# Full-width summary scores and another order of the first batch in a sparse-attention and mixture-of-experts kernel

## The chip, the core and the metric

The kernel runs on one core of a Trainium2 chip. The metric is device time in microseconds of one execution. Of several executions the median is taken.

## The reference

Two layers follow each other. The first is sparse attention with 4 batches, 8 heads, 768 positions and a head dimension of 64. Each query sees the keys that are less than 16 positions away, and in addition one summary of each block of 32 positions: the summary key is the maximum over the block, the summary value is the mean, and log 32 is added to its score.

```python
k_sum = k.reshape(B, H, nb, 32, D).max(axis=3)      # 24 summaries per head
v_sum = v.reshape(B, H, nb, 32, D).mean(axis=3)
scores_l = scale * q @ k.T                           # kept where |i - j| < 16
scores_s = scale * einsum('bhsd,bhnd->bhsn', q, k_sum) + log(32)
a = softmax(concat([scores_l_masked, scores_s]))
x = a @ concat([v, v_sum])                           # then (3072, 512)
```

The second is a mixture of 8 experts, each of them applied to all 3072 tokens and weighted by a routing matrix P that eight Sinkhorn steps make out of `exp(x @ w_gate)`.

```python
for e in range(8):
    out += P[:, e:e+1] * (relu(x @ w1[e]) @ w2[e])   # 512 -> 1024 -> 512
```

## The kernel before

Attention goes by pairs of heads: 16 pairs, four to a batch. A pair is one group of 128 partitions (two heads of 64). The first batch is cut into halves of 384 positions: four pairs, first halves, then the same four pairs, second halves (`pair_half`). The twelve pairs of the other batches are done whole (`pair_whole`). Between the attention work the kernel puts the products of expert 0 (`hidden0`, L211, and `project0`, L216), which need only the positions that are done. After the last attention come the Sinkhorn steps and experts 1 to 7, whose products follow Strassen's scheme (L764 and L815) with sums of weights, of tokens and of hidden values made on VectorE.

The steps of a pair, with the letter that the orders below use for its first half and the line of the profile:

- T, Q: keys and queries are transposed on TensorE (L300, L303, L312). k, q: the copies out of PSUM (L207), on ScalarE or VectorE.
- m: the key maxima over blocks of 32 on VectorE (L335, 128x24).
- v, V: block sums of the values on TensorE (L357) and their copy on VectorE (L363).
- S, X, b: scores of the near keys on TensorE (L347, in 64-row tiles), their exponentials on ScalarE (L490 for halves, L408 for whole pairs) and the band mask on VectorE (L495 and L500, or L412).
- s, e: summary scores on TensorE and their exponentials on ScalarE (L472).
- A, n: the products with the values on TensorE (L512 for halves, L435 and L441 for whole pairs) and the normalisation on VectorE (L542, L543).
- t, x: the transposition of the result (L550) and its copy to `xT` (L207).

Digits are the pair's number in its batch. F is a filler of zeros on TensorE; further fillers (`FILL`) are written into the first steps of v, S and s.

Summary scores have three forms. `summaries` for first halves uses 64x32 tiles (L452). For second halves it uses one matmul with all 128 columns of `ksT` (L455), where VectorE's `key_max_split` (L341) has put the maxima of the two heads into columns 0 to 63, each head's at its own 64 rows and zeros elsewhere, and columns 64 to 127 are zero. `summaries_2`, for the twelve whole pairs, runs two matmuls of 64 columns and 384 queries each, one for each half of the queries, into partitions 0 to 63 and 64 to 127 of one bank (L461). `summary_exp` then reads each half into rows 0 to 63 of `E_e`.

PSUM has three banks under tag "m" (products of expert 0, and the first halves' transpositions and summaries), three under "a" (the other attention steps) and one pair of banks under "s" (scores).

What sets the order: each step is added to a planner (`Plan`) with an engine or a choice of engines, a cost in microseconds, its dependencies, its buffers and a priority. `order` places the steps one after another where they can start first, and the program is written in that order, so that every engine's queue is fixed. Where a step may run on ScalarE or VectorE, the planner chooses. For the first halves of the first batch the order on TensorE, VectorE and ScalarE is written out by hand and made binding with `follow`:

```python
for u, d in zip(units, [None] + units):
    u.eng = {eng: u.eng[eng]}
    if d is not None:
        u.deps.append(d)
```

Of the kernel before, what the change touches and what calls it, by code (L numbers as in the profile page):

```python
# [10 lines left out]
BF16 = mybir.dt.bfloat16  # L11
# [117 lines left out]
def kernel(  # L129
# [10 lines left out]
    nc = tc.nc  # L140
# [12 lines left out]
    W = 16  # L153
    LIVE = 128 + 2 * W
    PADL = LIVE + 2 * W
    HS = S // 2
# [64 lines left out]
    NB = PB  # L221
# [4 lines left out]
    with tc.manual_schedule():  # L226
        attn = stage.enter_context(tc.tile_pool(name="attn", bufs=1))
# [10 lines left out]
        qT = [attn.tile([128, W + S + W], BF16, name=f"qT{i}") for i in range(NB)]  # L238
        kT = [attn.tile([128, S], BF16, name=f"kT{i}") for i in range(NB)]

        ks = [attn.tile([128, 1, 32], BF16, name=f"ks{i}") for i in range(NB)]
        ksT = [attn.tile([128, 128], BF16, name=f"ksT{i}") for i in range(NB)]
        v_x = [attn.tile([128, 2, G, VD], BF16, name=f"vx{i}") for i in range(NQ)]

        E_h = [attn.tile([128, 2, HG + 1, PADL], BF16, name=f"Eh{i}") for i in range(NEH)]
# [16 lines left out]
        def bank(tag, name, dtype=FP32):  # L262
            pool, n = (mps, 3) if tag == "m" else (aps, NA)
            return pool.tile([128, 2048 // mybir.dt.size(dtype)], dtype, tag=tag, name=name, bufs=n)
# [73 lines left out]

        def key_max_split(i):
            r = i % NB  # L340
            nc.vector.tensor_tensor(out=ksT[r][:, 0:64].rearrange("p (j n) -> p j n", j=2),  # L341
                                    in0=ks[r][:].to_broadcast([128, 2, 32]),
                                    in1=own[:].to_broadcast([128, 2, 32]), op=ALU.mult)

# [99 lines left out]
        def summaries(i, h, tag):  # L444
            r = i % NB
            ss, rhs = bank(tag, "ss"), qT[r][:, W + h * HS:W + (h + 1) * HS]
            wait_busy("s", i, h, ss)
            at["ss", i, h] = ss
            if i < PB and not h:
                for j in range(2):  # L450
                    p = slice(64 * j, 64 * j + 64)
                    nc.tensor.matmul(ss[32 * j:32 * j + 32, 0:HS], lhsT=ks[r][p, 0, :], rhs=rhs[p],  # L452
                                     start=True, stop=True)
                return
            nc.tensor.matmul(ss[:, 0:HS], lhsT=ksT[r][:], rhs=rhs, start=True, stop=True)  # L455

        def summaries_2(i):
            r, ss = i % NB, bank("a", "ss")
            for h in range(2):
                at["ss", i, h] = ss[64 * h:64 * h + 64]  # L460
                nc.tensor.matmul(ss[64 * h:64 * h + 64, 0:HS], lhsT=ksT[r][:, 0:64],  # L461
                                 rhs=qT[r][:, W + h * HS:W + (h + 1) * HS], start=True, stop=True)

        def summary_exp(i, h):
            if i < PB:
# [155 lines left out]
        def wait_busy(what, i, h, t):  # L621
            for _ in range(FILL.get(what + str(i), 0) if i < PB and not h else 0):
                stream(t, 512)
# [29 lines left out]
        def constants():  # L653
            nc.vector.memset(warm, 0.0)
            nc.scalar.dma_start(out=wg_f32[:], in_=moe_w_gate.rearrange("(dk p) e -> p dk e", p=128))
            nc.scalar.activation(out=warm[:], in_=warm[:], func=AF.Exp, bias=0.0, scale=1.0)
            for t in qT:
                nc.vector.memset(t[:, 0:W], 0.0)
                nc.vector.memset(t[:, W + S:], 0.0)
            for t in qT:  # L660
                nc.vector.memset(t[:, W + HS:W + HS + W], 0.0)
            for t in ks:
                nc.vector.memset(t[:, 0, 24:32], 0.0)
            for t in ksT:
                nc.vector.memset(t[:, 64:128], 0.0)
            for t, n in ((own, 64), (own_n, 32)):
                nc.vector.memset(t, 0.0)
                for j in range(2):
                    nc.vector.memset(t[n * j:n * j + n, j, :], 1.0)
            for t in E_h:  # L670
                nc.vector.memset(t[:, :, :, 0:W], 0.0)
                nc.vector.memset(t[:, :, :, W + LIVE:], 0.0)

            nc.vector.memset(m_blk, 0.0)
            flat = m_blk[:].rearrange("p g n -> p (g n)")
            for pq in range(4):
                for o in (pq, 32 + pq):
                    nc.vector.memset(flat[32 * pq:32 * pq + 32, o:o + 132 * (G - 1) + 1:132], 1.0)
            summary_constants(0)

        def summary_constants(i):
            t = V_s[i]
            nc.vector.memset(t[:], 0.0)
            nc.vector.memset(t[0:24, D:VD], 32.0)
            nc.vector.memset(t[32:56, VD + D:2 * VD], 32.0)
# [195 lines left out]
        def pair_start(i, prio):  # L881
            o = i - NB
            war_k = [U.get(("S", o, 0)), U.get(("S", o, 1)), U.get(("km", o))]
            war_q = war_k[:2] + [U.get(("ss", o, 0)), U.get(("ss", o, 1))]
            ahead = U.get(("S", i - 1, 1 if i > PB else 0))
            if i >= BY_DMA:
                for z in range(2):
                    U["tr", i, z] = add("SP", 1.4, lambda z=z: tr_dma(i, z),
                                        [U["kq"[z], i], U.get(("S", i - 3, 1))] + (war_k, war_q)[z], prio)
                    U["kT", i, z] = add("DMA", 1.7, None, [U["tr", i, z]], prio, lag=2.0)  # L890
            for z in range(0 if i >= BY_DMA else 1 if i < PB else 2):
                buf = Buffer("m" if i < PB else "a")
                U["tr", i, z] = add("PE", 0.5 if i < PB else 0.34, lambda z=z: tr(i, z),
                                    [U["kq"[z], i], U["ident"]] + (war_k, war_q)[z]
                                    + [U["tr", i, 0] if z else ahead], prio, opens=[buf])
                U["kT", i, z] = add({"ACT": 0.8, "DVE": 0.95 if i < PB else 0.56}, 0,
                                    lambda z=z: tr_out(U["kT", i, z].on, i, z), [U["tr", i, z]], prio,
                                    uses=[buf])
            U["ks", i] = add("DVE", 0.95, lambda: key_max(i), [U["kT", i, 0], U.get(("km", o))], prio)
            if i >= PB:  # L900
                U["km", i] = add("DVE", 0.23, lambda: key_max_split(i), [U["ks", i]] + war_q[2:], prio)
            buf = Buffer("a")
            U["vs", i] = add("PE", 0.4, lambda: block_sums(i),
                             [U["v", i]] + ([U.get(("A", i - NE, 1)), U["vc", i % NE]] if i >= PB else []), prio + 0.01, opens=[buf])
            sc = add("DVE", 0.25, lambda: summary_constants(i), [], prio - 1.0) if 0 < i < PB else None
            U["Vs", i] = add("DVE", 0.28 if i < PB else 0.7, lambda: block_out(i), [U["vs", i], sc],
                             prio + 0.01, uses=[buf])

        def pair_half(i, h, prio):
            n = PB * h + i  # L910
            hold = U["xt", PB - 1, 0] if h else None
            if h:
                U["km", i] = add("DVE", 0.23, lambda: key_max_split(i), [U["no", PB - 1, 0]], prio)
# [12 lines left out]
                                [U["X", i, h], U["band"], hist("A", n - NEH)], prio)  # L926
            buf = Buffer(tag)
            U["ss", i, h] = add("PE", 0.17 if h else 0.25, lambda: summaries(i, h, tag),
                                [U["km" if h else "ks", i], U["kT", i, 1 + h], hist("A", n - 2)], prio, opens=[buf])
            U["sx", i, h] = add("ACT", 0.46, lambda: summary_exp(i, h), [U["ss", i, h]], prio, uses=[buf])  # L930
# [13 lines left out]
        def pair_whole(i, prio):  # L944
# [17 lines left out]
            for h in range(2):  # L962
# [3 lines left out]
                             [U["X", i, 0], U["X", i, 1], U["mk", i, 1], U.get(("A", i - NE, 1)), U["ec", i % NE]], prio)  # L966
            buf = Buffer("a")
            U["ss", i, 0] = U["ss", i, 1] = add("PE", 0.22, lambda: summaries_2(i),
                                                [U["km", i], U["kT", i, 1], U.get(("A", i - NE, 1))], prio, opens=[buf])
            for h in range(2):  # L970
# [90 lines left out]
        for i in range(PB):  # L1061
# [11 lines left out]
        U["fill"].opens[0].users.append(U["fill"])  # L1073
        first["F"] = lambda i: U["fill"]
        plan.follow("PE", [first[c[0]](int(c[1])) for c in
                           "T0 F0 Q0 v0 S0 T1 Q1 s0 S1 T2 Q2 s1 A0 S2 v1 T3 Q3 A1 s2 S3 t0 v2 v3 t1 s3 A2 A3 t2 t3".split()])
        plan.follow("DVE", [first[c[0]](int(c[1])) for c in
                            "m0 V0 k1 m1 b0 q2 b1 n0 V1 m2 b2 n1 m3 V2 b3 V3 n2 n3 x3".split()])
        plan.follow("ACT", [first[c[0]](int(c[1])) for c in
                            "k0 q0 X0 q1 e0 X1 k2 e1 X2 k3 q3 X3 e2 x0 e3 x1 x2".split()])  # L1080
        expert0(0, [U["x", i, 0] for i in range(PB)])
        for i in range(PB):
            pair_half(i, 1, 10 + i)
# [237 lines left out]
```

## Time and profile before

| | |
|---|---|
| median of 4 runs | 667.93 us (667.61 to 668.11) |
| the profiled execution | 668.01 us |
| its span, first to last instruction | 666.3 us |
| granted TensorE clock | 1.00 |
| TensorE busy | 657.8 us, 99% of the span |
| VectorE busy | 546.8 us, 82% |
| ScalarE busy | 414.2 us, 62% |
| GpSimd busy | 199.3 us, 30% |
| bytes moved by DMA | 67.89 MB, 102 GB/s on average |

The time is that of the whole execution; the span leaves out some 1.7 us around the first and last instruction. PE stands for TensorE's matmuls, PEld for its weight loads, DVE for VectorE, ACT for ScalarE, POOL for GpSimd, SP for SyncE. Matmuls are pipelined, and a matmul's row shows its whole latency: the start of the next one says how long TensorE was taken up, not the end. A row with "x6" stands for six instructions in succession. What stands in square brackets is the time for which the engine was idle before, and what ended that.

### The profile page before, as it was taken

What the parts mean: (1) busy time and instruction counts of PE and PEld (TensorE: products, weight loads), DVE (VectorE), ACT (ScalarE), POOL (GpSimd) and SP (SyncE); (2) the same over time, 40 slices, a digit from 0 to 9 for tenths busy, and PEclk for the clock granted to TensorE, in tenths of its full rate; (3) what the DMA queues carried; (4) which work ended last, traced back from release to release, by engine and by line L of the source; (5) the groups of instructions that cost most, each with busy time, mean ns of one, the idle gap of its engine ahead of it and who ended that gap; (6) DMA issues with size and microseconds to landing.
All of it is one profiled execution on the core that took longest, in us unless ns stands there. A gap on an engine that the chain in (4) does not pass through costs nothing.

```text
span 666.3 us, 13254 instructions
## 1 busy us (share of the span) xinstructions
PE 657.8 (99%) x5131; PEld 434.5 (65%) x5132; DVE 546.8 (82%) x1029; ACT 414.2 (62%) x774; POOL 199.3 (30%) x257
## 2 busy tenths in 40 slices
PE   8999999999999999999999999999999999999997
PEld 4666655555676666666666666666666666666666
DVE  7889887799979787888789887888778877988776
ACT  5777875566876666556565665656565656556652
POOL 8899523000132222222221222222122213222123
PEclk9999999999999999999999999999999999999999
DMA  9999932700863747473754756373837465334656
GB/s 163 185 147 143 141 70 42 127 0 1 136 107 61 128 69 123 75 127 64 100 99 70 129 79 109 67 126 63 129 64 128 79 95 96 64 64 111 155 136 202
DMA packets 112558, 67.89 MB, mean 102 GB/s; under 512 B 77936, under 2 KB 90480, under 8 KB 112496
## 3 DMA queue, kind: packets, MB, share of 16 engines
q0 software_dynamic: 94816, 57.46, 64.9%
q1 hardware_dynamic: 17152, 9.58, 5.9%
q8 instruction: 40, 0.66, 0.4%
q14 instruction: 22, 0.18, 0.1%
q10 hardware_dynamic: 528, 0.02, 0.0%
HBM read 52.45 MB, written 6.29 MB: 88 GB/s over the span
## 4 chain that ended last, share of the span: by engine, by line
PE 96%; DMA 1%; DVE 1%; ACT 1%; issue 0%; POOLq 0%; DVEq 0%
PE yps L815 22%; PE pA L764 22%; PE pY L815 17%; PE pQ L764 11%; PE hps L211 6%; PE yps L216 6%; PE pR L764 5%; PE sg L347 1%; DMA qst<-in_q_dram 1%; PE tkq L303 1%; PE vs L357 1%; PE av L512 1%; PE av L435 1%; PE av L441 1%; PE tx L550 1%; PE ss L461 1%
## 5 line engine op out<-in xcount | busy, mean ns | idle before, releaser
L815 PEld LDWEIGHTS <-h 128*128 128x128 f16 x2352 | 230.1, 98 | 89.4 <-issue 1.0
L843 POOL DMA_DIRECT2D out_acc<-y x120 | 101.7, 888 | 372.4 <-ACT y L839 118.3
L839 ACT ACTIVATE y<-pY,P_sb 128x256 f32<-128x256 f32 x168 | 80.1, 478 | 125.9 <-PE pY L815 123.7
L830 DVE SCALAR_TENSOR_TENSOR out_acc<-yps,P_sb,out_acc 128x512 f32<-128x512 f32 x128 | 95.3, 745 | 29.7 <-PE yps L815 29.7
L798 DVE TENSOR_TENSOR h<-h 128x1024 f16<-128x1024 f16 x168 | 109.1, 684 | 1.4
L815 PE MATMUL pY<-w,h 128*128 128x256 f16 x672 | 100.1, 273 | 0.6 <-ACT y L839 0.6
L764 PE MATMUL pA<-xT,w 128*128 128x512 f16 x336 | 98.3, 379 | 0.0
L815 PE MATMUL yps<-w2sum,h 128*128 128x256 f16 x672 | 98.0, 273 | 0.0
L815 PE MATMUL yps<-w,h 128*128 128x256 f16 x672 | 93.3, 273 | 0.0
L830 DVE SCALAR_TENSOR_TENSOR out_acc<-pY,P_sb,out_acc 128x512 f32<-128x512 f32 x84 | 62.9, 749 | 32.3 <-PE pY L815 30.7
L764 PEld LDWEIGHTS <-w 128*128 128x128 f16 x672 | 65.8, 98 | 31.2 <-issue 0.2
L764 PEld LDWEIGHTS <-w1sum 128*128 128x128 f16 x504 | 49.3, 98 | 44.8 <-issue 0.4
L786 DVE CUSTOM_DVE_ANT_0 h<-pQ,snap 128x512 f16<-128x512 f32 x84 | 57.7, 687 | 6.2 <-ACT snap L207 3.6
L786 DVE CUSTOM_DVE_ANT_0 h<-pA,snap 128x512 f16<-128x512 f32 x84 | 57.5, 684 | 5.5 <-PE pA L764 5.2
L202 ACT ACTIVATE h<-pA 128x512 f16<-128x512 f32 x84 | 50.6, 603 | 13.3 <-PE pA L764 13.2
L202 ACT ACTIVATE h<-pR 128x512 f16<-128x512 f32 x84 | 50.1, 597 | 8.5 <-PE pR L764 8.5
L815 PE MATMUL pY<-w2sum,h 128*128 128x256 f16 x336 | 50.4, 273 | 0.0
L207 ACT COPY pR<-pA 128x512 f32<-128x512 f32 x81 | 46.2, 570 | 6.6 <-PE pA L764 5.6
L764 PE MATMUL pQ<-xT,w1sum 128*128 128x512 f16 x168 | 50.0, 379 | 0.2 <-ACT snap L207 0.2
L764 PE MATMUL pA<-xsum,w 128*128 128x512 f16 x168 | 50.0, 379 | 0.0
L764 PE MATMUL pR<-xT,w 128*128 128x512 f16 x168 | 50.0, 379 | 0.0
L764 PE MATMUL pA<-xsum,w1sum 128*128 128x512 f16 x168 | 50.0, 379 | 0.0
(150 smaller groups left out, 852.2 us busy)
## 6 DMA issues: line engine op xcount, KB each, us to landing
out_acc<-y POOLq DMA_DIRECT2D x120, 256.0 KB, 3.4
w<-in_moe_w_dram POOLq DMA_DIRECT2D x14, 1024.0 KB, 10.3
out_dram<-out_acc SPq DMA_DIRECT2D x24, 256.0 KB, 2.4
qst<-in_q_dram POOLq DMA_DIRECT2D x32, 96.0 KB, 5.4
vx<-in_v_dram POOLq DMA_DIRECT2D x15, 192.0 KB, 6.4
kst<-in_k_dram POOLq DMA_DIRECT2D x24, 96.0 KB, 5.6
w<-in_moe_w_dram POOLq DMA_DIRECT2D x4, 256.0 KB, 7.1
w<-in_moe_w_dram POOLq DMA_DIRECT2D x2, 512.0 KB, 8.1
```

The source lines that it names most:

```text
L202: nc.scalar.activation(out=out, in_=in_, func=AF.Relu, bias=0.0, scale=1.0)
L207: (nc.scalar.copy if eng == "ACT" else nc.vector.tensor_copy)(out=out, in_=in_)
L211: nc.tensor.matmul(hp[:, 0:n], lhsT=w1s[e][:, dk, f * 128:(f + 1) * 128], rhs=xT[:, dk, t0:t0 + n], start=(dk == 0), stop=(dk == KD - 1))
L216: nc.tensor.matmul(yp[:, d], lhsT=h[:, f, c * 128:(c + 1) * 128], rhs=w2s[e][:, f, d], start=(f == 0), stop=(f == KF - 1))
L303: nc.tensor.transpose(t[:, g * 128:(g + 1) * 128], st[:, g, :, :].rearrange("p j d -> p (j d)"), ident)
L764: nc.tensor.matmul(dst[:], lhsT=lhsT, rhs=rhs, start=first and k == 0, stop=k == HK - 1, skip_group_check=True)
L786: nc.vector._custom_dve(dve_ops.TENSOR_ADD_SAT, out=ring(e, p, q)[:, q % 2, blk, :], in0=at[src, e, p, q][:], in1=at.pop(("snap", n, e, p, ...
L798: nc.vector.tensor_tensor(out=h[:, :, out_, :], in0=h[:, :, a, :], in1=h[:, :, b, :], op=op)
L815: nc.tensor.matmul(dst[:, d], lhsT=lhsT, rhs=rhs, start=f == 0 and n in (1, 5, 2), stop=f == HF - 1, skip_group_check=True)
L830: nc.vector.scalar_tensor_tensor(out=o, in0=y, scalar=scalar, in1=o, op0=ALU.mult, op1=ALU.add)
L839: nc.scalar.activation(out=at[key][:, d], in_=src, func=AF.Copy, bias=0.0, scale=P_sb[:, t, e:e + 1])
L843: nc.gpsimd.dma_start(out=o, in_=at.pop(("y", e, p, c, key))[:], accum_op=ALU.add)
```

## The change

It has two parts. In the summary scores of whole pairs the maxima now lie in columns 64 to 127 of a `ksT` of 192 columns, with zeros on both sides. Each of the two matmuls takes 128 columns, for the first half of the queries columns 64 to 191 (maxima, zeros), for the second columns 0 to 127 (zeros, maxima), and both accumulate into the same bank, so that each half's scores land in the same partitions as before. `summaries` takes columns 64 to 191. In the first batch the three written orders are others.

```diff
-        ksT = [attn.tile([128, 128], BF16, name=f"ksT{i}") for i in range(NB)]
+        ksT = [attn.tile([128, 192], BF16, name=f"ksT{i}") for i in range(NB)]
...
         def key_max_split(i):
             r = i % NB
-            nc.vector.tensor_tensor(out=ksT[r][:, 0:64].rearrange("p (j n) -> p j n", j=2),
+            nc.vector.tensor_tensor(out=ksT[r][:, 64:128].rearrange("p (j n) -> p j n", j=2),
...
-            nc.tensor.matmul(ss[:, 0:HS], lhsT=ksT[r][:], rhs=rhs, start=True, stop=True)
+            nc.tensor.matmul(ss[:, 0:HS], lhsT=ksT[r][:, 64:192], rhs=rhs, start=True, stop=True)
 
         def summaries_2(i):
             r, ss = i % NB, bank("a", "ss")
             for h in range(2):
                 at["ss", i, h] = ss[64 * h:64 * h + 64]
-                nc.tensor.matmul(ss[64 * h:64 * h + 64, 0:HS], lhsT=ksT[r][:, 0:64],
-                                 rhs=qT[r][:, W + h * HS:W + (h + 1) * HS], start=True, stop=True)
+                nc.tensor.matmul(ss[:, 0:HS], lhsT=ksT[r][:, 64 - 64 * h:192 - 64 * h],
+                                 rhs=qT[r][:, W + h * HS:W + (h + 1) * HS], start=h == 0, stop=h == 1)
...
             for t in ksT:
-                nc.vector.memset(t[:, 64:128], 0.0)
+                nc.vector.memset(t[:], 0.0)
...
         plan.follow("PE", [first[c[0]](int(c[1])) for c in
-                           "T0 F0 Q0 v0 S0 T1 Q1 s0 S1 T2 Q2 s1 A0 S2 v1 T3 Q3 A1 s2 S3 t0 v2 v3 t1 s3 A2 A3 t2 t3".split()])
+                           "T0 F0 Q0 v0 S0 T1 Q1 s0 S1 T2 Q2 s1 A0 S2 v1 T3 A1 Q3 s2 t0 S3 v2 t1 s3 v3 A2 A3 t2 t3".split()])
         plan.follow("DVE", [first[c[0]](int(c[1])) for c in
-                            "m0 V0 k1 m1 b0 q2 b1 n0 V1 m2 b2 n1 m3 V2 b3 V3 n2 n3 x3".split()])
+                            "m0 V0 k1 m1 b0 q2 b1 n0 V1 m2 b2 n1 m3 x1 V2 b3 V3 n2 n3 x3".split()])
         plan.follow("ACT", [first[c[0]](int(c[1])) for c in
-                            "k0 q0 X0 q1 e0 X1 k2 e1 X2 k3 q3 X3 e2 x0 e3 x1 x2".split()])
+                            "k0 q0 X0 q1 e0 X1 k2 e1 X2 k3 q3 x0 e2 X3 e3 x2".split()])
```

## Prediction

> **What bounds the kernel now.** I read the page first, then the chain of waits in order of time, then TensorE's timeline around the summary matmuls, and last VectorE's busy time in the attention stage.
>
> ```profile
> PE 657.8 (99%) x5131; PEld 434.5 (65%) x5132; DVE 546.8 (82%) x1029; ACT 414.2 (62%) x774; POOL 199.3 (30%) x257
> ...
> PE 96%; DMA 1%; DVE 1%; ACT 1%; issue 0%; POOLq 0%; DVEq 0%
> ```
>
> TensorE carries 96% of the chain that ends last, so a change pays in three ways only: less TensorE time, fewer waits of TensorE, or an earlier start of its unbroken stretch. The profiled execution took 668.01 us (span 666.3); the median of the four is 667.93. About 0.2% (1.3 us) is what a measurement of this kernel can tell from no change. TensorE's timeline shows what one pair of summary matmuls (L461) costs (start, duration, engine, line, operation, tiles, tile shape, output, count):
>
> ```profile
> 42.56 0.34 PE L441 MATMUL av<-Ve,Ee 128*128 128x130 bf16 x3
> 42.82 0.35 PE L461 MATMUL ss<-qT,ksT 128*64 128x384 bf16 x2
> 43.11 1.04 PE L216 MATMUL yps<-w,h 128*128 128x512 f16 x4
> 43.98 0.50 PE L303 MATMUL tkq<-ident,kst 128*128 128x128 bf16 x6
> ```
>
> Starts matter here, since matmuls overlap. From 42.56 to 43.98 are 1.42 us. Three matmuls of L441 take 0.17 and four of L216 take 0.86 where the tile shape does not change (chain of waits), so the pair costs 0.39. The two 64-column halves do run together: four 384-column matmuls take 0.65 (next fence), 0.163 each, and the pair streams for 0.16, not 0.32. The other 0.23 is the change of tile shape, into 128x64 (0.09) and out again (0.13 to the next start, then 0.01). The chain shows the same price after the 64-row scores:
>
> ```profile
> 45.15 0.65 PE hps L211 x4
> ...
> 46.79 0.31 PE sg L347 x6
> 47.10 2.06 PE hps L211 x12
> ```
>
> Twelve at 0.163 are 1.95; the 0.11 on top is one change of shape. The last places to read are those where TensorE waited. In the attention stage there is one cluster, in the chain of waits:
>
> ```profile
> 63.31 0.17 PE av L441 x3
> 63.48 0.33 PE sg L347 x6
> 63.81 0.02 issue
> 63.84 0.97 ACT er L408
> 64.81 0.70 ACT kT L207
> 65.51 0.05 issue
> ```
>
> Two score groups that follow closely share the two banks of tag "s"; the second waits for ScalarE to empty them. Between TensorE's starts this cost about 0.7 us. The other, in the expert stage, is 0.4 us between starts:
>
> ```profile
> 181.49 0.60 PE L815 MATMUL pY<-w,h 128*128 128x256 f16 x4
> 182.33 0.59 PE L764 MATMUL pQ<-xT,w1sum 128*128 128x512 f16 x2 [0.24 <-ACT snap L207]
> ```
>
> **Full-width summaries.** Twelve pairs become 24 matmuls of full shape. Streaming: 24 x 0.163 = 3.90 in place of 12 x 0.16 = 1.92, so +1.98 us. The changes of shape are counted from the order of both built programs: 118 before, 98 after, 20 fewer. By the pair above one is worth 0.23 / 2 = 0.115, so -2.30. Sum: -0.3 us. Bounds: at 0.09 each it is +0.2, at 0.13 it is -0.6. Nine of the twelve pairs of before stand between full-shape work, where all of 0.39 - 0.325 = 0.065 is saved; next to scores one change of shape remains. I take -0.3, as 0.115 is this very instruction's row.
>
> The Trainium skill, "TensorEngine Tiling (Array Packing)", Overview, speaks against this half of the change: outputs of 64 columns or fewer are to be packed into column tiles for up to twice the speed. The trace agrees that the halves overlap. The same page's Key Properties say that a change of tiling mode drains the engine, without a figure; the measured 0.23 per pair is what decides. By the first rule alone the sum would be about +2 us, by the row it is -0.3.
>
> The exponential of the first half (0.48 on ScalarE) now waits for both matmuls, 0.16 later. The values that use it stand at least 1.3 us of TensorE work behind the pair's start in the new order, and it needs 0.33 + 0.48, so this is hidden; without that cover it is at most 0.16 for each of 12 pairs, 1.9. The wider memsets of ksT add some 0.05 x 4 = 0.2 us to VectorE before 6 us, where it then idles 1.4 us for the first values; hidden, and 0.2 if not.
>
> **The first batch.** Before, TensorE runs Q3, A1, s2, S3, t0, v2, v3, t1, s3, A2; after, A1, Q3, s2, t0, S3, v2, t1, s3, v3, A2. What it did:
>
> ```profile
> 16.54 1.15 PE L357 MATMUL vs<-vx,m_blk 128*128 128x128 bf16 x12
> 17.57 0.33 PE L550 MATMUL tx<-ident_x,xs 128*128 128x128 f16 x3
> 17.83 0.34 PE L452 MATMUL ss<-qT,ks 64*32 64x384 bf16 x2
> 18.31 0.63 PE L512 MATMUL av<-vx,Eh 128*128 128x65 bf16 x16
> ...
> 21.15 0.33 PE L550 MATMUL tx<-ident_x,xs 128*128 128x128 f16 x3
> ```
>
> Two waits of about 0.3 and 0.2 lie here: inside the first row v3 waits until 17.18 for the fourth pair's values, which land at 17.05, and A2 waits until 18.31 for a bank that ScalarE's copy x0 frees at 18.27. After, t1 and s3 stand between v2 and v3, and x0 comes ahead of e2 and X3 on ScalarE, so both go. By hand, with the rows' durations: A1 14.30, Q3 15.14, s2 15.77, t0 16.05, S3 16.32 (its queries' copy, 0.48, ends at 16.2), v2 16.65, t1 16.99, s3 17.39 (the fourth key maximum ends 17.32), v3 17.67, A2 18.05. But X3 now starts at 17.2 instead of 16.53, its masks end at 18.96, and A3 starts at 19.37 against 19.32, with three hidden-layer pieces done ahead of it instead of one. Then t3 needs the normalisation behind A3 (0.14 + 0.56 us on VectorE after 20.3), so it starts near 21.15 in both, with six pieces done in both. What is late next is thus A3's normalisation, and the gain is 0. Bounds: -0.3 (t3's wait filled otherwise) to +0.4 (x1, now on VectorE, holds up V2 and the masks). GpSimd's queue keeps its order. On SyncE's queue one to two transposes of the thirteenth and fourteenth pairs (1.2 to 2.4 us each) move ahead of the near values of the eleventh and twelfth; those are issued at 69.1 and 74.4 us and used at 82.5 and 88.0, so this is hidden, and would cost up to 3.6 us without that slack.
>
> **Everything behind it.** The planner places all later work from these starts, so TensorE's order differs in the first 4,230 of its 10,242 instructions. Summing the rows' durations along both orders, the two closest score groups stand 1.43 us of TensorE work apart before (the cluster above) and 1.76 after, so that wait of 0.7 has reason to go. The last logits stand 1.9 us later, but the first product that needs a sum of weights keeps, by a sum of VectorE's rows, 0.5 us of slack. New waits can't be read from a trace of another order. The nearest row is before's own: 0.7 + 0.4 us of waits between 20 and 640 us. I take the same again for the new order, so 0, with bounds -1.1 (none) and +1.8 (next part).
>
> Sum: 668.01 - 0.3 = 667.7 on the profiled execution, which is 0.1 above the median: 667.6 us.
>
> **Rivals.** *VectorE becomes the bound (slower).* Some evacuations move from ScalarE to VectorE. Between the sixth and the tenth normalisation VectorE was already this busy (stretch, length, then PE, PEld, DVE, ACT, POOL busy, clock, DMA):
>
> ```profile
> 31.10:44.10 13.00, 13.00 (x165) 8.05 (x164) 10.17 (x28) 9.54 (x16) 13.00 (x17) 1.00 2.27 149
> ```
>
> ```profile
> 34.22 0.29 DVE L363 TENSOR_TENSOR Ve<-vs,own_n 64x128 bf16<-64x128 f32 x1 [0.40 <-PE vs L357]
> ...
> 38.39 0.56 DVE L207 COPY kT<-tkq 128x768 bf16<-128x768 bf16 x1 [0.71 <-PE tkq L303]
> ```
>
> That is 2.83 us idle. After, the same stretch of the order (11.8 us of TensorE work, 11.6 before) holds one key maximum (0.95), two copies to out_acc (0.69 each) and one hidden copy (0.56) more, and one copy to xT (0.36) and one split of maxima (0.22) fewer: +2.3. 0.5 us of idle time is left, and what idle there was came as waits for TensorE. If those stay, TensorE waits 2.3 - 0.5 = 1.8 us: 668.0 - 0.3 + 1.8 = 669.5. It decides from the point where less than 1.8 of the 2.83 us can be filled. For it: five idle pieces of 0.2 to 0.7, each ended by another engine. Against it: ScalarE is relieved by the same copies, and behind the tenth normalisation the new order is looser (32.4 us of VectorE work in 34.6 of TensorE's up to the twentieth, 29.2 in 30.0 before).
>
> *The waits go and none come (faster).* 668.0 - 0.3 - 0.7 - 0.4 = 666.6. For it: the wider spacing of the scores. Against it: in the expert stage nothing in the edit touches the wait at 182 us.
>
> *The change of shape is not saved.* If a full matmul behind scores pays as much as a pair did, the 1.98 us of streaming remain: 670.0. Against it: the lone full-shape matmul of L455 between full-shape work at 31.25 cost 0.17.
>
> **How the numbers follow.** Forecast (shape changes saved, waits as before, 667.6): 0.45. Waits gone, 666.6 or less: 0.20, on the edge of 0.2% and so counted as faster. VectorE, or a wait like it elsewhere in the new order, 669.5: 0.28. Shape not saved, 670.0: 0.07. So faster 0.20, same 0.45, slower 0.35. The range runs from just under the fast case, 666.4, to between the two slow ones, 669.8. The forecast's own range is 667.2 to 668.4.
>
> **What would show it.** Right: L461 at shape 128*128 with starts 0.16 apart, and the work behind it without 0.11 on top; t3 near 21.15; no idle VectorE of note between 32 and 44 us and no wait of TensorE there; no wait for ScalarE between the two score groups of one pair. Wrong: TensorE waiting for VectorE's xs, em or h in the attention stage (slower), or no wait over 0.2 us up to 640 us (faster); A2 not before 18.2 would show that the hand sum of the first batch fails.

## The result, and the profile after

After the change the median is 666.96 us (666.61 to 670.85, 45 runs), before it 668.00 (667.51 to 670.67, 69 runs). The ratio is 0.9987, 95% interval 0.9983 to 0.9991: 0.6 to 1.1 us faster. That lies inside the range given and, by the bound of 0.2%, in the class "same", 0.6 us below the forecast of 667.6. It is also below the forecast's own narrower range of 667.2 to 668.4. The profiled execution took 666.63 us, the third fastest of the 45; its span is 664.8. Of all executions reported in this document one, of the new head below, took 3894 us for no recorded reason, and no ratio counts it.

The page of the profile after, busy times first, then the chain that ended last:

```profile
PE 657.6 (99%) x5131; PEld 435.9 (66%) x5132; DVE 550.4 (83%) x1034; ACT 411.9 (62%) x769; POOL 198.8 (30%) x257
...
PE 95%; DVE 3%; DMA 1%; issue 0%; ACT 0%; POOLq 0%; DVEq 0%
```

TensorE's busy time is the same to 0.2 us. VectorE has 3.6 us more of it and ScalarE 2.3 less: the planner moved evacuations, and VectorE now has 3% of the chain where it had 1%. TensorE's timeline around one pair of summary matmuls (start, duration, line, tiles, tile shape, count):

```profile
59.85 0.50 PE L303 MATMUL tkq<-ident,qst 128*128 128x128 bf16 x6
60.19 0.49 PE L461 MATMUL ss<-qT,ksT 128*128 128x384 bf16 x2
60.52 1.89 PE L216 MATMUL yps<-w,h 128*128 128x512 f16 x8
```

Shape 128*128, and 0.33 from start to start where the old pair took 0.39. The first batch in the same view:

```profile
16.16 0.52 PE L357 MATMUL vs<-vx,m_blk 128*128 128x128 bf16 x6
16.52 0.33 PE L550 MATMUL tx<-ident_x,xs 128*128 128x128 f16 x3
16.91 0.34 PE L452 MATMUL ss<-qT,ks 64*32 64x384 bf16 x2
17.18 0.52 PE L357 MATMUL vs<-vx,m_blk 128*128 128x128 bf16 x6
17.53 0.63 PE L512 MATMUL av<-vx,Eh 128*128 128x65 bf16 x16
...
20.65 0.34 PE L550 MATMUL tx<-ident_x,xs 128*128 128x128 f16 x3
```

v2, t1, s3, v3 and A2 follow each other without the two old waits. Each starts 0.47 to 0.52 earlier than in the hand sum (t1 was put at 16.99, A2 at 18.05), and so does t3: this execution's first values reached TensorE 0.47 us earlier (v0, the first L357, at 7.63 instead of 8.10). The window of the clock that the VectorE rival read (length, then PE, PEld, DVE, ACT, POOL busy):

```profile
31.10:44.10 13.00, 13.00 (x184) 8.82 (x182) 11.90 (x31) 8.13 (x14) 12.82 (x16) 1.00 2.22 145
```

VectorE is busy for 11.90 us in place of 10.17, and TensorE for all 13.00. The same stretch of the order, from the end of the sixth normalisation to the end of the tenth, runs from 30.77 to 43.70 us and ran from 31.55 to 44.06 before: VectorE is busy for 11.83 of 12.93 us there, in place of 9.72 of 12.51. The list of TensorE's waits between 20 and 640 us is empty; by the starts, 0.21 us are left ahead of the logits at 66.0 and 0.29 at 179. The first of them is a wait for VectorE, as the chain of waits shows:

```profile
65.70 0.48 DVE xT L207
66.18 0.04 issue
66.22 0.74 PE lp L570 x24
```

### The profile page after: what moved, and what is told of

Read it like the earlier page. It is cut to its first block, busy times and chain, and to the rows that moved or that the text cites. A ratio compares the mean times of both kernels' runs of the same rounds, so it can differ in the third digit from the quotient of the medians.

```text
span 664.8 us, 13246 instructions
## 1 busy us (share of the span) xinstructions
PE 657.6 (99%) x5131; PEld 435.9 (66%) x5132; DVE 550.4 (83%) x1034; ACT 411.9 (62%) x769; POOL 198.8 (30%) x257
## 4 chain that ended last, share of the span: by engine, by line
PE 95%; DVE 3%; DMA 1%; issue 0%; ACT 0%; POOLq 0%; DVEq 0%
PE yps L815 22%; PE pA L764 22%; PE pY L815 17%; PE pQ L764 11%; PE hps L211 6%; PE yps L216 6%; PE pR L764 5%; PE sg L347 1%; DMA qst<-in_q_dram 1%; PE vs L357 1%; PE av L512 1%; PE tkq L303 1%; PE av L435 1%; DVE xs L543 1%; PE ss L461 1%; PE av L441 1%
## 5 line engine op out<-in xcount | busy, mean ns | idle before, releaser
L843 POOL DMA_DIRECT2D out_acc<-y x120 | 101.4, 888 | 372.4 <-ACT y L839 98.4
L764 PE MATMUL pQ<-xsum,w1sum 128*128 128x512 f16 x168 | 50.0, 379 | 0.0
```

The lines of the kernel that those rows point to most:

```text
L764: nc.tensor.matmul(dst[:], lhsT=lhsT, rhs=rhs, start=first and k == 0, stop=k == HK - 1, skip_group_check=True)
L843: nc.gpsimd.dma_start(out=o, in_=at.pop(("y", e, p, c, key))[:], accum_op=ALU.add)
```

## The experiments

Run times of this kernel scatter by more than the parts are worth, but the starts in a trace do not. Three places cut each profiled execution, and the table has a row for each kernel whose parts can be compared. The three are v0 (the first L357), t3 (the last first-half transposition, L550) and the last matmul.

| kernel | v0 at | v0 to t3 | t3 to the last matmul |
|---|---|---|---|
| before | 8.10 | 13.05 | 640.65 |
| width alone | 7.63 | 13.31 | 640.22 |
| new tail | 7.64 | 13.51 | 640.22 |
| before, Q0 late | 8.63 | 13.05 | 640.63 |
| after | 7.63 | 13.02 | 639.66 |
| order alone | 7.63 | 13.01 | 640.18 |
| new head | 7.63 | 13.02 | 641.24 |
| after, Q0 late | 8.87 | 13.03 | 639.67 |
| A3 earlier | 7.62 | 12.85 | 639.90 |
| t2 earlier | 7.63 | 12.76 | 639.66 |

The new head takes 13.01 to 13.03 us in each of its four rows. Behind t3, kernels that share their order agree within 0.04 us, with two exceptions. The new head's last column, which should be before's, holds 0.60 at 554.6 us where ScalarE waited for one late accumulate DMA of the expert stage (L843). A3 earlier, which should have after's, holds 0.24 more, as its own lines show below. The old head does not repeat: it takes 13.05 to 13.51.

The theories: A, fewer shape changes, and the score wait near 64 us goes, while the first batch gives nothing; B, the two waits of the first batch are the gain; C, the width is all of it.

**Order alone**: the kernel before with the three new `follow` strings.

```diff
-  "... T3 Q3 A1 s2 S3 t0 v2 v3 t1 s3 A2 A3 t2 t3"
+  "... T3 A1 Q3 s2 t0 S3 v2 t1 s3 v3 A2 A3 t2 t3"
...
```

> The three written orders of after, with the 64-column summary pairs of before. Theory A (two causes that add up: 20 changes of tile shape fewer, worth 0.3 us, and the wait of 0.7 us between two score groups that the new order behind the first batch takes away; the first batch itself gives nothing): 0.5 us under before, 667.5. Theory B (the first batch's own two waits of 0.3 and 0.2 us are the gain): also 0.5 under, 667.5. Theory C (the width does it all): as before, 668.0.

Measured: 667.60 us, ratio 0.9996 (0.9987 to 1.0005). The chain of waits around the two score groups:

```profile
62.91 0.31 PE sg L347 x6
...
64.89 0.31 PE sg L347 x6
65.20 0.44 PE tx L550 x6
```

**Width alone**: the changed kernel with the three old strings, so the same lines with plus and minus exchanged.

> Full-width summaries in before's order. The changes of tile shape fall from 118 to 97: 24 x 0.163 - 12 x 0.16 - 21 x 0.115 = -0.4 us. Theory A: 0.3 to 0.4 us under before, and the wait between two score groups near 64 us still in the trace. Theory B: 0.4 under. Theory C: 0.9 under before, 667.1.

Measured: 667.86 us, 0.9999 (0.9991 to 1.0008). Its chain at the same place:

```profile
63.16 0.33 PE sg L347 x6
63.49 0.02 issue
63.52 0.97 ACT er L408
64.49 0.70 ACT kT L207
65.19 0.05 issue
65.23 0.38 PE sg L347 x6
```

The run times can't separate the two. The traces can: the wait for ScalarE stays with the width and goes with the order. In this view the groups start 1.98 us apart with TensorE's own work in between, and 2.07 apart with the wait inside. Behind t3 the order alone gains 0.47 (640.65 to 640.18) and the width alone 0.43 (640.22), in the new order 0.52 (640.18 to 639.66). C falls, and so does B as a full account.

**New head** and **new tail**: the kernel before, with the planner's places 93 to 158 (up to t3) or 159 to 1404 taken from the changed kernel and all others as before.

```diff
-        for u in plan.order():
+        done = plan.order()
+        for n, p in enumerate("...".split()):      # unit:engine, from the changed kernel's order
+            i, e = p.split(":")
+            done[93 + n] = plan.units[int(i)]      # 159 for the tail
+            done[93 + n].on = e
+        for u in done:
```

> Before's kernel with 64-column pairs, in which only the 66 planner places up to the fourth pair's first transposed result (t3) stand as in after; every later place stands as in before. Theory A: as before, 668.0, and t3 no earlier relative to the first queries. Theory B: 0.5 us under before. Theory C: as before.

> The counterpart: the first batch up to t3 as in before, every later place as in after, 64-column pairs. Theory A: 0.5 us under before, 667.5, without the wait between two score groups near 64 us. Theory B: as before, 668.0. Theory C: as before.

Measured: head 668.34 us, 1.0007 (0.9998 to 1.0016); tail 667.92, 0.9996 (0.9984 to 1.0008). By run time neither differs from before. By the trace the tail gains 0.43 behind t3, and the new head is the shorter one: 13.02 against 13.31 and 13.51. Where the old head loses it when v0 is early, the list of TensorE's waits of the new tail shows (total, times, longest), and the timeline of width alone; both run the old head:

```profile
PE tkq L312 <- DMA qst<-in_q_dram: 0.4, 1, 0.4
PE vs L357 <- DVE Vs L363: 0.4, 1, 0.4
```

```profile
16.15 0.51 PE L357 MATMUL vs<-vx,m_blk 128*128 128x128 bf16 x6
17.23 0.50 PE L357 MATMUL vs<-vx,m_blk 128*128 128x128 bf16 x6 [0.57 <-DMA vx<-in_v_dram]
```

In one Q3 waits for the fourth pair's queries, and v3 for a bank that VectorE then frees late; in the other v3 waits for the fourth pair's values. These land at 17.09 us in width alone and at 17.05 in before, though its v0 is 0.47 later. So the old order, begun early, asks for the transfers earlier, and they don't land earlier. In the profiled execution of before v0 itself was late, and these waits were shorter. The size of the loss differs with the landings: in the new tail the fourth queries land at 14.25, in the other thirteen traces at 13.05 to 13.96.

The new head is not free of this. With v0 near 7.63 it starts v3 at 17.17 or 17.18 if the values are there. Three further profiled executions with its order up to v3 had them later: at 17.24 (A3 earlier), 17.31 (the doubled copy) and 17.75 (WHOLE = 8), with v3 at 17.29, 17.36 and 17.79. From v0 to t3 the last two took 13.19 and 13.63.

**Price of the shape, five times over**: each pair of summary matmuls five times, with one full matmul between one pair and the next, in the wide and in the narrow form, both in the new order.

```diff
-            for h in range(2):
-                ...
+            for n in range(9):
+                if n % 2:
+                    nc.tensor.matmul(ss[:, 0:HS], lhsT=<128 columns>, rhs=qT[r][:, W:W + HS], start=True, stop=True)
+                    continue
+                for h in range(2):
+                    ...
```

> The changed kernel with each pair of full-width summary matmuls run five times, with one further full matmul of 384 queries between one pair and the next: 12 x (4 x 2 + 4) = 144 more matmuls of full shape. Theory A (TensorE's time counts one to one and full matmuls cost 0.1625 us each): 144 x 0.1625 = +23.4 us, 690.4. Rival H (such work fills waits or hides behind VectorE): at least 1 us less. To be read against the next kernel.

> The new orders with the old pairs of 64 columns (the kernel of order alone), each pair run five times with the same full matmul between one pair and the next, so that every pair stands between full-shape work. Theory A (a pair costs 0.39 there, 0.16 of streaming and 0.23 for the two changes of shape): +12 x 4 x (0.39 + 0.1625) = +26.5 us on 667.6, 694.1, and the wide kernel is faster by about 3.7 us (60 pairs x 0.065, less some at scores). Rival C (a change of shape costs nothing where it recurs, only the streaming counts): 667.6 + 12 x 4 x 0.325 = 683.2, 7 us faster than the wide kernel. Rival D (a pair costs the same in both forms, the gain of the edit is the order alone): 690.4 to 691, within 0.6 of the wide kernel.

Measured: wide 691.22 us (four runs: 690.21 and 690.32, 692.12 and 692.30; nothing recorded explains the two groups; the profiled one is the first), narrow 694.04 (693.68 to 694.08). The timelines, wide first:

```profile
37.45 0.33 PE L461 MATMUL ss<-qT,ksT 128*128 128x384 bf16 x1
37.62 0.49 PE L466 MATMUL ss<-qT,ksT 128*128 128x384 bf16 x2
37.94 0.33 PE L461 MATMUL ss<-qT,ksT 128*128 128x384 bf16 x1
```

```profile
37.35 0.34 PE L461 MATMUL ss<-qT,ksT 128*128 128x384 bf16 x1
37.62 0.35 PE L466 MATMUL ss<-qT,ksT 128*64 128x384 bf16 x2
37.90 0.34 PE L461 MATMUL ss<-qT,ksT 128*128 128x384 bf16 x1
```

One full matmul and one pair take 0.49 wide (37.45 to 37.94) and 0.55 narrow (37.35 to 37.90). From t3 to the last matmul the wide kernel needs 662.99 us, 23.33 more than after (expected 23.4); the narrow one 666.67, 26.49 more than order alone (expected 26.5). The difference is 3.68 for 60 pairs; by the medians of the run times it is 2.8, against the lower two of the wide runs 3.8. Per matmul that is 23.33 / 144 = 0.162, and per narrow pair 26.49 / 48 - 0.162 = 0.390. A holds, its three rivals fall, and the added TensorE time counted one to one.

**Q0 held back** in the changed kernel and in the one before, by a longer filler F0.

```diff
-        U["fill"] = add("PE", 0.64, lambda: keep_busy(512, 256), [], 0, opens=[Buffer("m")])
+        U["fill"] = add("PE", 0.64, lambda: keep_busy(*8 * [512]), [], 0, opens=[Buffer("m")])
```

> The changed kernel with eight instead of one and a half filler matmuls ahead of the first transposed queries (Q0), so that Q0 starts near 7.5 us as in the profiled execution of before, whenever the queries land. Theory E (the new first batch follows Q0 almost one to one, the old one is held by the fourth pair's values and by ScalarE's copy x0 whenever Q0 comes): t3 at 21.05 to 21.2 in place of 20.65, 0.4 to 0.5 us slower than the changed kernel's 667.0, that is 667.4. Rival F (the new order gains 0.5 us wherever Q0 stands): t3 at 20.65 to 20.75 and the time of the changed kernel.

> The same longer filler in the kernel before. Theory E: t3 at 21.1 to 21.2, where it is at 20.94 to 21.15 without the filler; at most 0.2 us slower than before. Rival F: t3 0.4 to 0.5 later, near 21.5, and 0.4 us slower than before.

Measured: after 667.39 us, 0.9990 (0.9981 to 0.9999); before 668.51, 1.0007 (0.9999 to 1.0016). The delay came out longer than planned, with Q0 at 8.33 and 8.10 instead of 7.5, so t3 is at 21.89 and 21.68, and the expected places are missed. The profiled execution of after with this filler took 668.04 us against a median of 667.39, so it was delayed more than most of its runs. Read from v0, the new head takes 13.03, as without the filler, and the old one 13.05, as in the late profile of before and 0.26 to 0.46 less than in its two early ones. So theory E holds for the new head. For the old one, by its four traces, it holds only up to a v0 near 8.1, behind which this head follows as well. That the old kernel lost 0.5 us fits this; for its time rival F, with 0.4, was nearer than E with at most 0.2.

**VectorE's slack**: the changed kernel with the copy L367 of each whole pair twice.

```diff
-                nc.vector.tensor_copy(out=ve[0:64, 1:G, :], ...)
+                for _ in range(2):
+                    nc.vector.tensor_copy(out=ve[0:64, 1:G, :], ...)
```

> The changed kernel with VectorE's copy L367 (0.48 us a row, some 0.40 from start to start) run twice for each of the twelve whole pairs: 12 x 0.40 to 0.48 = 4.8 to 5.8 us more VectorE work between 35 and 114 us, where the changed kernel leaves VectorE 7.85 us idle in 75.8. Theory A (VectorE is ahead of what TensorE needs, its idle time can be filled): under 0.5 us slower than the changed kernel, no wait of TensorE for VectorE over 0.2 us. Rival V (the VectorE rival of the prediction: the idle time is itself waits for TensorE, and added work comes out at the end): 3 to 5 us slower, with TensorE waiting for VectorE's xs, em, Ve or Ee.

Measured: 669.80 us, 1.0028 (1.0016 to 1.0040), against 0.9987 for the changed kernel: 2.7 us slower. From t3 to the last matmul it is 3.1, of which 0.2 are one wait in the expert stage. The list of TensorE's waits (total, times, longest):

```profile
PE lp L571 <- DVE xT L207: 0.9, 1, 0.9
PE ss L462 <- DVE ksT L341: 0.2, 1, 0.2
PE tkq L303 <- DVE rc L543: 0.2, 1, 0.2
```

Two copies take 0.92 from start to start where one takes 0.41, so 12 x 0.41 to 0.51 = 4.9 to 6.1 us were added, and about half of it came out at the end. It lies between A and V: VectorE has some slack left in the new order, but less than its idle time shows.

**Fewer shape changes still**: the changed kernel with another size.

```diff
-    WHOLE = 12
+    WHOLE = 8
```

> The changed kernel with WHOLE = 8 in place of 12: the pairs 8 to 11 run both score groups as one (two banks of tag a besides the pair of tag s), as pairs 12 to 15 do. The built order has 90 changes of tile shape in place of 98. Theory A (a change is worth 0.115 us of TensorE's time): 8 x 0.115 = -0.9 us, 666.0, if the two banks bring no wait. Rival W (three banks of tag a are then too few around the scores, TensorE waits for ScalarE's exponentials): slower, by 0.5 to 1 us for each of the four pairs, 668 to 670.

Measured: 668.45 us, 1.0007 (0.9995 to 1.0019), 1.3 us slower than the changed kernel. The rival is right about the sign and mostly wrong about the engine. The list of waits between 20 and 640 us, then the one wait for a transfer that the list from 10 to 120 us adds:

```profile
PE tx L550 <- DVE xs L543: 0.8, 3, 0.4
PE pY L815 <- ACT y L839: 0.6, 1, 0.6
PE ss L461 <- DVE ksT L341: 0.5, 1, 0.5
PE av L435 <- ACT xT L207: 0.4, 1, 0.4
```

```profile
PE vs L357 <- DMA vx<-in_v_dram: 0.5, 1, 0.5
```

Two of these are late transfers, and no run shows that the edit made them late. The values of the fourth pair, issued at 9.46 us as in after, landed 0.97 later than there, which took 0.61 us from v0 to t3. The second line is the accumulate DMA of the new head's trace once more: it took 12.5 us to land, where it took 11.5 in after, and TensorE lost 0.72 us at 555.8. Without the latter this kernel takes 1.52 us more than after from t3 to the last matmul. In the attention stage TensorE waits for VectorE (1.3 us) and once for a copy on ScalarE (0.4), not for the exponentials that the rival named. So the new order that the planner makes from this one number runs TensorE mainly into VectorE, which fits the run before, and the eight changes saved (0.9 us) don't pay for it.

**A3 earlier** and **t2 earlier**: places moved by hand in the planned order of the changed kernel, to fill t3's last wait of 0.29. The diff gives the order on TensorE that results; p is a hidden-layer piece (L211).

```diff
-  PE: ... A2 p p p A3 p t2 p p t3        # the changed kernel
+  PE: ... A2 p A3 p p p t2 p p t3        # A3 earlier
+  PE: ... A2 p A3 t2 p p p p p t3        # t2 earlier
```

> The changed kernel with two of the three hidden-layer pieces that stand between A2 and A3 in the first batch put behind A3; every other engine keeps its order. Theory A (t3 waits 0.29 us for the normalisation behind A3, which can start 0.33 earlier): A3 at 18.54 in place of 18.86, t3 at 20.38 in place of 20.65, its wait gone, and 0.27 us less on the whole, 666.4 in the profiled execution against 666.63. Rival (A3 then waits for the fourth pair's values, which VectorE writes at 18.66): the wait moves ahead of A3, and t3 stays at 20.55 to 20.65.

> The changed kernel with one hidden-layer piece between A2 and A3 in the first batch and the transposition t2 directly behind A3, ahead of the next five pieces; every other engine keeps its order. Theory A (what held t3 was A3's normalisation, and what held the pieces behind t3 in the run before was ScalarE's copy x2, 0.48 us behind a late t2): t2 at 19.48, t3 at 20.47, the pieces behind it at 20.64 with no wait, and from the first values on TensorE (v0) to its last matmul 652.40 us in place of 652.68; 666.35 to 666.4 in a profiled execution like that of the changed kernel. Rival (another step of the head is late next, as in the run before): 652.6 to 652.8 and no gain. The run times can hardly tell 0.28 us; the trace can.

Measured: A3 earlier 667.08 us, 0.9980 (0.9967 to 0.9994); t2 earlier 666.81, 0.9982 (0.9969 to 0.9994). A3 earlier gains nothing from v0 to the end (652.75 against after's 652.68), though 0.11 of it is the late landing of the values told above. TensorE's timeline, then ScalarE's copy x2:

```profile
19.98 0.33 PE L550 MATMUL tx<-ident_x,xs 128*128 128x128 f16 x3
20.15 0.49 PE L211 MATMUL hps<-xT,w 128*128 128x384 f16 x2
20.47 0.33 PE L550 MATMUL tx<-ident_x,xs 128*128 128x128 f16 x3
20.88 0.65 PE L211 MATMUL hps<-xT,w 128*128 128x384 f16 x3
```

```profile
20.35 0.48 ACT L207 COPY xT<-tx 128x384 f16<-128x384 f16 x1 [2.29 <-PE tx L550]
```

The wait moved behind t3 (20.64 to 20.88): the next pieces need x2, which ends at 20.83, and t2 stood behind pieces. Neither theory had named that; the next run was built on it, and its timeline shows the wait gone:

```profile
18.37 0.34 PE L211 MATMUL hps<-xT,w 128*128 128x384 f16 x1
18.54 0.63 PE L512 MATMUL av<-vx,Eh 128*128 128x65 bf16 x16
19.11 0.34 PE L512 MATMUL av<-Vs,es 64*128 64x130 bf16 x3
19.41 0.34 PE L550 MATMUL tx<-ident_x,xs 128*128 128x128 f16 x3
19.59 0.98 PE L211 MATMUL hps<-xT,w 128*128 128x384 f16 x5
20.40 0.33 PE L550 MATMUL tx<-ident_x,xs 128*128 128x128 f16 x3
20.57 0.65 PE L211 MATMUL hps<-xT,w 128*128 128x384 f16 x3
```

From v0 to the last matmul are 652.42 us (expected 652.40), 0.26 less than in the changed kernel. It is the shortest of all by the trace; the run times don't tell it from the changed kernel.

## Why the prediction was right or wrong

**The forecast's time was near, its account was not.** It had -0.3 for the width and 0 for everything else. The traces give -0.4 to -0.5 for the width, about -0.5 for the order behind the first batch, and between 0 and -0.5 for the first batch. All three parts lie on the fast side. The stated range holds the measured time because its fast end came from the rival in which the waits go, and not because of the forecast's own sum.

**Width: right mechanism, mis-sized term.** Under amplification a full matmul took 0.162 (0.163 in the sum) and a narrow pair 0.390 (0.39). The count was off. The 20 changes saved came from the whole programs, where the new order adds two of its own: 118 before, 120 in order alone, 98 after. The width's own count behind t3 is 21 in the old order (83 to 62) and 22 in the new (84 to 62): 21 x 0.115 - 1.98 = -0.43 and 22 x 0.115 - 1.98 = -0.55, measured -0.43 and -0.52. "The shape is not saved" falls by the same rows. The packing advice of the Trainium skill ("TensorEngine Tiling (Array Packing)", Overview), up to twice the speed, would have made the narrow kernel of 60 pairs up to 9.8 us faster than the wide one (60 x 0.163), an estimate from that page. By the traces it was 3.7 slower: each pair stands alone and pays 0.23 for the way in and out.

**First batch: the hand sum holds, its starting point did not.** The step "t3 starts near 21.15 in both, the gain is 0" is confirmed for its execution: with v0 at 8.1 or later both heads take 13.02 to 13.05. But that execution had late first queries, which hid what the old order pays when they come early: 0.29 in one trace, 0.49 in another. It was the odd one: of the twelve profiled executions without the long filler it alone has v0 at 8.10, the others at 7.62 to 7.81. "What is late next is A3's normalisation" is confirmed in the changed kernel by t3's wait of 0.29, and its cause by the last run.

**"The same waits again" is the step that failed.** The two score groups were summed to stand further apart, "so that wait of 0.7 has reason to go", and then the forecast kept it. It went: by the starts, 0.68 us ahead of the second score group are gone in order alone, 0.15 ahead of the logits are new, and in the expert stage 0.40 at 182 us became 0.29 near 180; with one more change of shape (0.115) the net is -0.53 by this sum, -0.47 as measured. A named wait whose cause the edit visibly moves should have been priced at its removal.

**The rivals.** "The waits go and none come" (666.6) describes the result best, though the wait of the expert stage went only in part. VectorE as the bound did not come: its stretch of the order took +2.1 us (+1.7 in the same window of the clock) instead of +2.3 and kept 1.1 idle instead of 0.5, without a wait of TensorE. What came of it is the 0.21 us ahead of the logits. The doubled copy shows how near it was: of the 4.9 to 6.1 us that it added, about half was paid.

**Open.** The parts in the traces add up to -1.0 with late and to -1.3 to -1.5 us with early first values; the runs say 0.6 to 1.1 faster. Eleven early starts in twelve traces speak against late starts as the whole reason. The profiled execution of after lies 0.33 under the median of its runs, and single late transfers took 0.1 to 0.7 us from four of the traces; what the untraced runs lost, and where, was not measured.

## What to carry to other kernels

Price a narrow tile shape by its neighbours: alone between full-shape work, this pair of half-width matmuls cost more than the same work at full width with zeros. Check which late transfer the profiled execution happened to have before a hand sum starts from it, and cut each trace at a few fixed instructions: where no transfer was late these repeated to a few hundredths of a microsecond, while run times scatter by over a microsecond. An order that fills one engine's idle time spends the slack of another, so measure what that engine has left before the next edit leans on it.

## What the runs showed of the hardware

The first queries, issued at 1.36 us in both, landed at 7.52 us in the profiled execution of before and at 6.87 in that of after; in the other twelve traces they landed at 6.61 to 7.23. The two longer fillers overshot mainly because TensorE was still slow when they began, in TensorE's timelines of after and of after with Q0 late:

```profile
5.33 0.53 PE L300 MATMUL tkq<-ident,kst 128*64 128x128 bf16 x12
```

```profile
5.47 0.85 PE L300 MATMUL tkq<-ident,kst 128*64 128x128 bf16 x12 [0.18 <-ACT kst L207]
```

In both, 512-column fillers start 0.43 apart up to 4.66 us and 0.21 to 0.23 apart later, but the step comes before 5.4 us in one and near 6.8 in the other. The granted clock reads 1.00 throughout, but the record behind this column has its first entry, at full rate, only at 5.14 us in the one and at 6.79 in the other; where the record is empty the column reads 1.00. In all fourteen traces the first matmul starts at 1.26 or 1.27 us and this entry lies between 3.91 and 7.23. The Trainium skill ("TensorE: Matmul & The Clock Gate", What's actually happening) tells of a cold half rate whose end varies from run to run. The starts (0.43, then 0.21 to 0.23) and the first entries agree with that; the clock column alone does not show it.
